# Inducing-point attention with a one-expert MLP on one Trainium2 core: second-pass weights exponentiated where the matmul leaves them, and gates of the last batch in sets of three groups

## The chip, the cores and the metric

One NeuronCore of a Trainium2 chip. The metric is device microseconds (us) of one execution; the kernel before has a median of 232.93 us over 3 runs (232.25 to 233.02). Everything is float32.

## The reference

Four batches of 11456 tokens with 128 features, and 32 inducing points. Two attention blocks follow each other, then a mixture of 8 experts:

```
h   = softmax(I @ x.T / sqrt(128)) @ x          # per batch: 32 x 128
out = softmax(x @ h.T / sqrt(128)) @ h          # per token, over the 32 rows of h
logits = out @ w_gate ; e = argmax(logits) ; gate = max softmax(logits)
y   = gate * (relu(out @ w1[e]) @ w2[e])
```

The inputs make the softmaxes nearly flat, so that all tokens of a batch take the same expert, and no hidden unit changes its sign within a batch. The kernel uses both: per batch it folds the expert into a 32-row matrix L, so that a token's output is (its 32 weights) @ L, scaled by a gate and the weights' sum. It checks what it assumes on the chip, and a flag sends it to a general path (`general_path`) where a check fails.

## The kernel before, in words

A batch is cut into 6 groups: five of 16 tiles of 128 tokens, and a last one of 10 tiles, two of them short. There are 24 groups in all.

**Pass 1** (`p1`, L393 on) per group: TensorE transposes the tiles (L404), a copy moves them from PSUM to `xT` (L406, through the helper at L317), four matmuls make the 32 scores of each token (L424), VectorE takes a maximum over each partition's scores (L431), TensorE spreads it (L435) and VectorE reduces it to one bias for each quadrant of 32 partitions (L438), ScalarE exponentiates (L442), VectorE transposes (L446), TensorE sums the weighted tokens (L453).

**Chain** (`chain`, L488) once per batch: combines the groups (L503 to L523), picks the expert (L527 to L533), gathers its weights by two indirect DMAs from GpSimd's queue (L539), and makes L (L574 to L598). L574 reads `w1e` through a view whose inner step is 8 floats.

**Pass 2** (`p2`, L607) per group: four matmuls make scores (L616) into one PSUM bank; VectorE transposes them in 32x32 blocks so that tokens lie on partitions (L618), takes each token's maximum (L620) and subtracts it (L622); ScalarE exponentiates in SBUF (L626); TensorE transposes back, four tiles at a time (L643); a copy moves the result to `eT` (L651); TensorE multiplies by L (L671); copies bring the products to `ys` (L713) and the group's gate is worked out (`gates`, L738: seven small instructions); GpSimd, ScalarE or VectorE scale (L724, L726), and a DMA stores (L734). In the last batch the logits have a matmul of their own (L654), so that the gates need not wait for L, the products are scaled straight out of PSUM (L702, L704) or, some of them, copied to `ya` and scaled by GpSimd (L695); it makes a set of gates for each group, and its stores go out four tiles at a time.

**Order.** All work is given to `Plan` (L130) as operations with a cost per engine, a key for their order, and the tiles that they open. `Plan.emit` runs a list scheduler over planned costs when the program is built; what it puts out is each engine's fixed order. It picks the engine too, where an operation names several (`Alt`), under offsets in `BIAS`. `BUFS` gives the buffers: 7 of `xT`, 6 of `x`. PSUM has 8 banks, and each tile that a matmul writes holds one until its last reader is done. SyncE issues the loads and stores in order.

Of the kernel before, what the change touches and what calls it, by code (L numbers as in the profile page):

```python
# [36 lines left out]
TM = 88  # L37
NMAIN = TM * 128
# [4 lines left out]
SCALE = 1.0 / math.sqrt(C)  # L43
OWN = -256.0
LAG = 7.38    
K1 = (-0.92, -2.62, -13.3, 1.06)
K2 = (-2.16, -2.56, 9.73, 0.73, 0.61, -2.99)
KC = -3    
XB = 0.58    
XR = 0.09      # L50
XS = 0.17    
XU = 0    
XV = 0    
XP = 50    
XW = 3
XG = 50    
XQ = (1, 1, 1, 2, 1, 0)
XH = 4
BIAS = {"tx": {"dve": 800, "act": -200}, "aT": {"dve": 100, "act": -300}, "hp": {"dve": 200, "act": -300}, "gq": {"dve": -100, "act": -100}, "s2s": {"dve": 500, "act": -200}, "eT": {"dve": 200, "act": 0}, "ys": {"dve": 0, "act": -100}, "eh": {"act": 0, "dve": 300}, "lo": {"pool": 0, "dve": 800, "act": 100}, "s1": {"pool": -200, "dve": 0, "act": -100}, "ld": {"pool": 1500, "dve": 0, "act": 50}, "yo": {"pool": 500, "dve": 300, "act": 500}, "s2s+": {"dve": -100, "act": 1500}, "eT+": {"dve": 0, "act": 50}, "ys+": {"dve": 0, "act": 50}, "eh+": {"act": 0, "dve": 200}, "lo+": {"pool": 0, "dve": 1500, "act": 50}, "s1+": {"pool": -200, "dve": -200, "act": 0}, "ld+": {"pool": 100, "dve": 0, "act": -200}, "yo+": {"pool": -200, "dve": 800, "act": 800}, "yy": {"dve": -100, "act": 100}, "hc": {"dve": 0, "pool": -300}, "yq": {"dve": 300, "act": 50}}
BUFS = {"w1e": 1, "w2e": 1, "x": 6, "xT": 7, "eT": 6, "sd": 4, "a": 1, "aT": 1, "ys": 3, "yo": 2}  # L60
# [3 lines left out]
def inducing_moe_kernel(ctx: ExitStack, tc: tile.TileContext, x, inducing, w_gate, w1, w2, out):  # L64
# [7 lines left out]
    def views(a, b, g):  # L72
        if g < G - 1:
            return [(0, 128, 0, 16, a[b, :NMAIN].rearrange("(p t) c -> p t c", t=TM)[:, g * 16:g * 16 + 16])]
        return [(0, 128, 0, 8, a[b, :NMAIN].rearrange("(p t) c -> p t c", t=TM)[:, 80:88]),
                (0, 64, 8, 10, a[b, NMAIN:NMAIN + 128].rearrange("(p q) c -> p q c", q=2)),
                (64, 128, 8, 9, a[b, NMAIN + 128:].rearrange("(p q) c -> p q c", q=1))]

# [11 lines left out]
    dve.memset(selx, 1.0)  # L90
# [12 lines left out]
    far = consts.tile([128, 128], F32, name="far")  # L103
    dve.tensor_scalar(far, sel4, 1e30, -1e30, op0=OP.mult, op1=OP.add)
# [13 lines left out]
    chk = consts.tile([128, B * G + B * NJ], F32, name="chk")  # L118
    flag = consts.tile([1, 1], I32, name="flag")

# [9 lines left out]
class Plan:  # L130
# [14 lines left out]
    WINDOW = 100  # L145
    SWITCH = 95

    def __init__(self):
        self.ops, self.tiles, self.pull, self.mode = [], {}, [], []
        self.log = []  # L150

# [3 lines left out]
    def op(self, engs, fn, r=(), w=(), key=0.0, hold=(), pull=0.0, mode=0):  # L155
# [7 lines left out]
    def emit(self, bufs, banks, run):  # L163
        n = len(self.ops)
        preds, users = [set() for _ in range(n)], {}
        writers, readers = {}, {}
        for i, (_, _, r, w, _, hold) in enumerate(self.ops):
# [16 lines left out]
        on = [None] * n  # L184
        left = {x: len(u) for x, u in users.items()}
        order = {}
        for i, (_, _, _, w, _, hold) in enumerate(self.ops):
            for x in w + hold:
                if x in self.tiles and self.tiles[x][0] != "bank":
# [6 lines left out]
        free_at = {t: [0.0] * bufs[t] for t in order}  # L196
        done, opened, last = [0.0] * n, {}, [[] for _ in range(banks)]
        bank_free = [0.0] * banks
        bank_of, bank_used = {}, [False] * banks
        clock = {"pe": 1100.0, "dve": 5300.0, "act": 2000.0, "sp": 1800.0}  # L200
        ready, cold, busy, mode = {i for i in range(n) if not need[i]}, 0.0, [], 0

        def slots(i):

            t, taken, more = [], [], []
            for x in self.ops[i][3] + self.ops[i][5]:
                if x not in self.tiles or x in opened:
                    continue
                tag = self.tiles[x][0]
                if tag == "bank":  # L210
                    k = pick(x, taken)
                    if k is None:
                        return None
                    taken.append(k)
                    t += last[k]
                else:
                    k = slot(tag, [u for g, u in more if g == tag]) if nxt[tag] + sum(g == tag for g, _ in more) == turn[x] else None
                    if k is None:
                        return None
                    more.append((tag, k))  # L220
                    t += users.get(holder[tag][k], ())
            return t

        def slot(tag, taken=()):

            free = [(free_at[tag][k], k) for k, y in enumerate(holder[tag]) if (y is None or not left[y]) and k not in taken]
            return min(free)[1] if free else None

        def pick(x, taken=()):

            allowed = range(4, banks) if x[0] == "y" else range(4) if any(self.mode[j] == 2 for j in ready) else range(banks)
            free = [k for k in allowed if not bank_used[k] and k not in taken]
            return min(free, key=lambda k: bank_free[k]) if free else None

        while ready:
            cand = []
            for i in ready:
                s0 = slots(i)
                if s0 is None:
                    continue  # L240
                for e, c in self.ops[i][0].items():
                    if e == "pe":
                        c *= 1.015
                    free = clock.get(e, 0.0) + (self.SWITCH if e == "pe" and self.mode[i] != mode else 0)
                    st = max([free] + [done[p] + self.edge(on[p], e) for p in s0]
                             + [done[p] + self.edge(on[p], e) for p in preds[i]])
                    if e == "pe" and (st < cold or st - clock[e] > 2200):
                        c *= 2
                    cand.append((st + getattr(self.ops[i][0], "bias", {}).get(e, 0.0) - self.pull[i], st, self.ops[i][4], i, st + c, e))
            first = min(cand)  # L250
            _, i, _, st, en, e = min((k, i, f, st, en, e) for f, st, k, i, en, e in cand
                                     if e == first[5] and f <= first[0] + self.WINDOW)
            engs, fn, r, w, _, hold = self.ops[i]
# [34 lines left out]
            for q in succs[i]:  # L288
                need[q] -= 1
                if not need[q]:  # L290
                    ready.add(q)
# [637 lines left out]
```

## Time and profile before

| | |
|---|---|
| median of 3 runs | 232.93 us (232.25 to 233.02) |
| the profiled execution's own time | 234.33 us |
| its span, first to last instruction | 232.5 us |
| mean granted TensorE clock | 0.900 |
| busy: TensorE, VectorE, ScalarE, GpSimd | 203.3, 175.0, 156.9, 75.8 us |
| read from and written to memory | 27.68 and 23.46 MB |

Busy is the time in which an engine had an instruction in work. For TensorE it is modelled, since its matmuls are pipelined. The profile's own time is 1.8 us over its span, and 1.4 us over the median of the runs.

### The profile page before, as it was taken

To read this page: it belongs to the slowest core of one execution; us is meant where nothing else is said; L and a number is where in the kernel's file an instruction comes from. 1 tells how busy PE (TensorE), PEld (TensorE's weight loads), DVE (VectorE), ACT (ScalarE), POOL (GpSimd) and SP (SyncE) were. 2 spreads that over 40 slices of the span, in tenths; PEclk is the share of its full clock that TensorE was granted. 3 is DMA by queue.
4 is the path that set the end of the run, shared out by engine and by line. 5 is a ranking of instruction groups with operands and counts; after the bars stand their busy time and mean duration, and the time that the engine had idled before them with its cause. 6 is when DMAs were issued, how large, how long until landed. Compare 5 with 4: busy or idle time off the path is not lost.

```text
span 232.5 us, 6577 instructions
## 1 busy us (share of the span) xinstructions
PE 203.3 (87%) x2510; PEld 135.4 (58%) x2510; DVE 175.0 (75%) x583; ACT 156.9 (67%) x429; POOL 75.8 (33%) x92
## 2 busy tenths in 40 slices
PE   8499997999999799899989989799989897799900
PEld 6277675457667474565766646375664365688700
DVE  4123284768489899998798899979897999987820
ACT  3268682186789778888976787696976876875410
POOL 2000000300014546853040477730157547712500
PEclk9979998599999999999999999999997998556655
DMA  6995759914337964959798086362005941866790
GB/s 206 375 407 206 273 180 379 307 59 123 94 149 234 395 230 169 382 206 401 223 307 318 9 259 285 148 261 66 4 39 191 312 185 66 341 240 227 266 336 25
DMA packets 12313, 51.65 MB, mean 222 GB/s; under 512 B 1617, under 2 KB 2673, under 8 KB 7921
## 3 DMA queue, kind: packets, MB, share of 16 engines
q1 hardware_dynamic: 11120, 46.95, 54.3%
q0 software_dynamic: 1152, 4.19, 5.9%
q8 instruction: 22, 0.36, 0.7%
q14 instruction: 19, 0.15, 0.2%
HBM read 27.68 MB, written 23.46 MB: 220 GB/s over the span
## 4 chain that ended last, share of the span: by engine, by line
PE 45%; DVE 36%; ACT 4%; issue 4%; DMA 3%; POOL 2%; SPq 1%; DVEq 0%; POOLq 0%; ACTq 0%
PE b L404 13%; PE b L453 7%; PE b L424 6%; PE b L671 6%; PE b L616 5%; DVE ys L317 4%; DMA x<-in_x_dram 3%; DVE sd L618 3%; DVE mx L620 3%; DVE sd L622 3%; DVE ld L749 2%; PE b L643 2%; DVE aT L446 2%; DVE mx L431 2%; PE b L435 1%
## 5 line engine op out<-in xcount | busy, mean ns | idle before, releaser
L726 POOL TENSOR_TENSOR yo<-ys,gs 128x512 f32<-128x512 f32 (+1 forms) x50 | 54.1, 1102 | 31.4 <-issue 14.2
L317 ACT COPY xT<-b 128x512 f32<-128x512 f32 (+1 forms) x92 | 49.1, 593 | 21.2 <-PE b L404 20.9
L404 PE MATMUL b<-ident,x 128*128 128x128 f32 x352 | 50.2, 289 | 3.8 <-DMA x<-in_x_dram 2.5
L404 PEld LDWEIGHTS b<-ident,x 128*128 128x128 f32 x352 | 41.4, 148 | 17.1 <-issue 7.5
L671 PE MATMUL b<-L,eT 32*128 32x137 f32 (+1 forms) x720 | 40.6, 325 | 1.1 <-DVE ys L317 0.6
L671 PEld LDWEIGHTS b<-L,eT 32*128 32x128 f32 x720 | 31.1, 206 | 17.7 <-issue 6.5
L317 ACT COPY ys<-b 128x274 f32<-128x274 f32 (+1 forms) x97 | 31.3, 388 | 9.0 <-PE b L671 7.4
L616 PE MATMUL b<-xT,hT 128*32 128x512 f32 (+1 forms) x192 | 26.6, 650 | 0.8 <-DVE sd L618 0.8
L453 PE MATMUL b<-x,aT 128*32 128x128 f32 x704 | 24.4, 277 | 1.6 <-DVE aT L446 1.2
L424 PE MATMUL b<-xT,IT 128*32 128x512 f32 (+2 forms) x192 | 24.1, 573 | 0.5 <-ACT xT L317 0.5
L746 POOL TENSOR_SCALAR s<-ys 128x16 f32<-128x16 f32 (+1 forms) x16 | 5.4, 340 | 57.2 <-DVE hp L484 24.1
L453 PEld LDWEIGHTS b<-x,aT 128*32 128x32 f32 x704 | 18.4, 110 | 8.1 <-PE b L424 1.9
L446 DVE STREAM_TRANSPOSE aT<-a 128x512 f32<-128x512 f32 (+1 forms) x24 | 16.1, 670 | 7.1 <-ACT a L442 6.6
L431 DVE TENSOR_REDUCE mx<-b 128x1 f32<-128x512 f32 (+1 forms) x24 | 15.4, 641 | 7.6 <-PE b L424 7.3
L618 DVE STREAM_TRANSPOSE sd<-b 128x512 f32<-128x512 f32 (+1 forms) x24 | 16.0, 668 | 4.9 <-PE b L616 4.9
L622 DVE CUSTOM_DVE_ANT_0 sd<-mx,sd 128x512 f32<-128x512 f32 (+1 forms) x24 | 19.0, 792 | 0.1
L442 ACT ACTIVATE a<-b,nb 128x512 f32<-128x512 f32 (+1 forms) x24 | 16.3, 678 | 4.0 <-DVE nb L438 4.0
L724 ACT ACTIVATE yo<-ys,gs 128x128 f32<-128x128 f32 x56 | 17.8, 399 | 0.9 <-ACT ys L317 0.8
L539 POOL DMA_INDIRECT w1e<-in_moe_w_dram,idx x4 | 4.4, 1101 | 41.1 <-DVE ei L535 39.7
L317 DVE COPY ys<-b 128x274 f32<-128x274 f32 x41 | 16.7, 427 | 0.8 <-PE b L671 0.7
L626 ACT ACTIVATE sd<-sd 128x512 f32<-128x512 f32 (+1 forms) x24 | 14.5, 615 | 3.1 <-DVE dst L622 3.0
L643 PE MATMUL b<-ident,sd 128*128 128x128 f32 (+1 forms) x92 | 15.3, 303 | 0.2 <-ACT sd L626 0.2
(189 smaller groups left out, 272.8 us busy)
## 6 DMA issues: line engine op xcount, KB each, us to landing
x<-in_x_dram SPq DMA_DIRECT2D x19, 1024.0 KB, 5.4
out_dram<-yo SPq DMA_DIRECT2D x15, 1024.0 KB, 4.3
out_dram<-ys SPq DMA_DIRECT2D x12, 256.0 KB, 3.4
out_dram<-yo SPq DMA_DIRECT2D x10, 256.0 KB, 2.7
x<-in_x_dram SPq DMA_DIRECT2D x4, 512.0 KB, 5.6
out_dram<-yo SPq DMA_DIRECT2D x3, 512.0 KB, 3.8
x<-in_x_dram SPq DMA_DIRECT2D x4, 256.0 KB, 3.4
xtail<-in_x_dram SPq DMA_DIRECT2D x4, 64.0 KB, 5.5
```

What stands on the lines that cost most here:

```text
L317: (eng.copy if eng is nc.scalar else eng.tensor_copy)(out, in_)
L404: e.transpose(T[t][:, k, :], xtile(i, t0 + k), ident) for k in range(n)],
L424: e.matmul(T[t][32 * k:32 * k + 32, :ends[k]], IT, T[xT][:, k, :ends[k]], start=True, stop=True) for k in range(4)],
L431: e.tensor_reduce(T[mx], T[t][:, :nt], axis=AX.XY, op=OP.max)
L446: plan.op({"dve": vec(w)}, lambda e: e.transpose(T[aT][:, :nt], T[a][:, :nt]), r=[a], w=[aT], key=base + K1[2], pull=pull)
L453: e.matmul(T[th][32 * k:32 * k + 32, :], T[aT][:n, q + k], xtile(i, q + k)[:n], start=q == 0, stop=q + k + 4 >= nt)
L616: e.matmul(T[tS][32 * k:32 * k + 32, :nt], hT, T[xT][:, k, :nt], start=True, stop=True) for k in range(4)],
L618: plan.op({"dve": vec(w)}, lambda e: e.transpose(T[s2][:, :nt], T[tS][:, :nt]), r=[tS], w=[s2], key=base + K2[0])
L622: plan.op({"dve": vec(w) + 10}, lambda e: e.tensor_tensor_reduce(out=T[sd][:, :nt, :], in0=T[mx][:, :nt].unsqueeze(2).to_broadcast([128, n ...
L643: e.transpose(T[t][:rows(a), a, :], T[sd][:, 4 * a:min(4 * a + 4, nt)].rearrange("p t m -> p (t m)"), ident)
L671: e.matmul(T[t[k]][:, a - q0, :], T[eT][32 * k:32 * k + 32, a, :], T[L][32 * k:32 * k + 32, :width], start=True, stop=True)
L726: e.tensor_mul(T[yo][:, t0:t0 + n], yv()[:, t0:t0 + n, :C], T[gs][:, t0:t0 + n].unsqueeze(2).to_broadcast([128, n, C]))
```

## The change

Pass 2 no longer brings the tokens to the partitions. The scores are made against `hq`, which is h less its mean, already multiplied by the scale; VectorE takes the largest absolute score of each partition, then of each quadrant of 32 partitions, and ScalarE exponentiates out of PSUM into `eT` with that as its bias. It writes `eT` in order, and reads the bank with an inner step of 32 floats. The transposes back and the copy to `eT` are gone. The tokens' places in a group are chosen so that this works: a load's partition holds 16 tokens in a row, a store's runs are of 4 tokens (2 in the last group). Pass 1 spreads its maximum by a VectorE transpose and four small matmuls. The gates' constant 1 is a ninth column of the exponentials. In the last batch one set of gates serves three groups, and stores are two to a group. The first three groups are loaded in four pieces each. The planner's constants, costs, buffers and offsets are new; it fills the gaps that it plans on TensorE with matmuls on ones. The core of the diff:

```diff
-BUFS = {"w1e": 1, "w2e": 1, "x": 6, "xT": 7, "eT": 6, "sd": 4, "a": 1, "aT": 1, "ys": 3, "yo": 2}
+BUFS = {'w1e': 1, 'w2e': 1, 'x': 5, 'xT': 9, 'eT': 5, 'a': 1, 'aT': 1, 'ys': 3, 'yo': 2}
+FILL = (320, 200)
+GL = 3
+EARLY = 3
...
+            if e == "pe" and st - clock[e] > FILL[0] and ops[i][0][e] > 60:
+                k = [k for k in range(banks) if not bank_used[k] and bank_free[k][1].get(e, 0.0) < clock[e] + 150]
+                if k:
+                    self.fill[i] = (max(k, key=lambda k: bank_free[k][0]), st - clock[e] - FILL[1])
...
+        if i < EARLY:
+            for t0 in range(0, 16, 4):
+                plan.op({"sp": 650}, lambda e, t0=t0: part(e, t0), key=i - 3 + 0.01 * t0,
+                        w=[("x", i), ("x", i, t0)] + ([] if i or t0 < 12 else ["ind"]))
...
-        plan.op({"pe": 109}, lambda e: e.transpose(T[tm], T[mx].to_broadcast([128, 128]), ident), r=[mx], w=[tm],
...
+        plan.op({"dve": 110}, lambda e: e.transpose(T[mm], T[mx].to_broadcast([128, M])),
...
+            e.matmul(T[tm][32 * k:32 * k + 32, :], T[mm], v["r4"], start=True, stop=True) for k in range(4)],
...
+        plan.op({"dve": 75}, lambda e: e.tensor_reduce(T[nb][:, g:g + 1], T[tm], axis=AX.X, op=OP.min),
...
-            w1v = T[w1e].rearrange("p (f j) -> p j f", j=NJ)
+            w1v = T[w1e].rearrange("p (f j) -> p f j", j=NJ)
...
+        def largest(e):
+            e.tensor_reduce(dst[:, b, g:g + 1], T[tS][:, :nt], axis=AX.XY, op=OP.max, apply_absolute_value=True)
+            e.transpose(T[mq], dst[:, b, g:g + 1].to_broadcast([128, 32]))
+            e.tensor_reduce(T[nq], T[mq], axis=AX.X, op=OP.max, negate=True)
...
+        def weights(e):
+            n = nt // 4 * 4
+            e.activation(T[eT][:, :n].rearrange("p (s i) j -> p s (i j)", i=4).rearrange("p s (j i) -> p s j i", i=4),
+                         T[tS][:, :n].rearrange("p (s i) j -> p s j i", i=4), AF.Exp, bias=T[nq])
+            for t in range(n, nt + nt % 4, 2):
...
+                e.activation(T[eT][:, t:t + 2], T[tS][:, n:nt], AF.Exp, bias=T[nq])
...
-        plan.op({"dve": vec(w)}, lambda e: e.transpose(T[s2][:, :nt], T[tS][:, :nt]), r=[tS], w=[s2], key=base + K2[0])
...
-            e.transpose(T[t][:rows(a), a, :], T[sd][:, 4 * a:min(4 * a + 4, nt)].rearrange("p t m -> p (t m)"), ident)
...
+            if o == GL - 1:
+                gates(i - o, 16 * o + 4 * ns, lambda: T[st], 0, [(st, k) for k in range(GL)], [st], base + K2[3], "+")
...
+                        for s in range(0, ns, 2):
+                            s1 = min(s + 2, ns)
+                            e.tensor_mul(part(yo, q, s, s1), part(ys, q, s, s1)[:, :, :C], times(q, s, s1))
...
+        step = 2 if last else 4
+        for q in range(0, 4, step):
+            def store(e, q=q):
+                e.dma_start(out=main[:, q:q + step], in_=yv()[:, q:q + step, :sm])
```

The check for the general path also asks that exp(-2 d) of the largest score d is at least 0.02 (`LEAST`).

## Rows read from the trace of the kernel before

**Rows 1.** Busy time of each engine in three stretches, with granted clock and DMA share
```profile
core 0: us, PE busy (x) PEld busy (x) DVE busy (x) ACT busy (x) POOL busy (x), PEclk, DMA share, GB/s
41.00:60.00 19.00, 19.00 (x177) 10.70 (x177) 13.51 (x43) 11.40 (x24) 2.11 (x2) 0.86 0.49 167
60.00:222.00 162.00, 148.98 (x1938) 99.39 (x1936) 144.30 (x479) 122.90 (x354) 72.07 (x79) 0.92 0.59 216
222.00:232.50 10.50, 0.00 (x0) 0.00 (x0) 0.28 (x1) 0.00 (x0) 0.00 (x0) 0.50 0.47 161
```

**Rows 2.** The chain that ended last, by engine and by line, from the page
```profile
PE 45%; DVE 36%; ACT 4%; issue 4%; DMA 3%; POOL 2%; SPq 1%; DVEq 0%; POOLq 0%; ACTq 0%
PE b L404 13%; PE b L453 7%; PE b L424 6%; PE b L671 6%; PE b L616 5%; DVE ys L317 4%; DMA x<-in_x_dram 3%; DVE sd L618 3%; DVE mx L620 3%; DVE sd L622 3%; DVE ld L749 2%; PE b L643 2%; DVE aT L446 2%; DVE mx L431 2%; PE b L435 1%
```

**Rows 3.** Busy time as in rows 1, of the last 26 us of work alone
```profile
196.00:222.00 26.00, 23.13 (x230) 19.51 (x230) 22.31 (x76) 16.85 (x51) 11.19 (x13) 0.57 0.71 270
```

**Rows 4.** Groups of instructions that pass 2 loses: count, busy us, mean ns, idle before
```profile
L618 DVE STREAM_TRANSPOSE sd<-b 128x512 f32<-128x512 f32 (+1 forms) x24 | 16.0, 668 | 4.9 <-PE b L616 4.9
L620 DVE TENSOR_REDUCE mx<-sd 128x16 f32<-128x512 f32 (+1 forms) x24 | 15.4, 641 | 0.1
L622 DVE CUSTOM_DVE_ANT_0 sd<-mx,sd 128x512 f32<-128x512 f32 (+1 forms) x24 | 19.0, 792 | 0.1
L626 ACT ACTIVATE sd<-sd 128x512 f32<-128x512 f32 (+1 forms) x24 | 14.5, 615 | 3.1 <-DVE dst L622 3.0
L643 PE MATMUL b<-ident,sd 128*128 128x128 f32 (+1 forms) x92 | 15.3, 303 | 0.2 <-ACT sd L626 0.2
L317 ACT COPY eT<-b 128x512 f32<-128x512 f32 (+2 forms) x19 | 10.3, 571 | 1.9 <-PE b L643 1.7
L317 DVE COPY eT<-b 128x512 f32<-128x512 f32 (+2 forms) x9 | 3.9, 457 | 0.5 <-PE b L643 0.5
```

**Rows 5.** Line L618 alone, from 60 us on: us, DVE busy (count), clock, DMA
```profile
60.00:222.00 162.00, 13.18 (x20) 0.92 0.59 216
```

**Rows 6.** Groups that price what the change adds: columns as in rows 4
```profile
L431 DVE TENSOR_REDUCE mx<-b 128x1 f32<-128x512 f32 (+1 forms) x24 | 15.4, 641 | 7.6 <-PE b L424 7.3
L471 DVE TENSOR_REDUCE nb<-nb 128x1 f32<-128x5 f32 x4 | 0.6, 154 | 0.1
L594 DVE COPY lq<-b 128x128 f32<-128x128 f32 x4 | 1.0, 258 | 0.8 <-PE b L591 0.8
L442 ACT ACTIVATE a<-b,nb 128x512 f32<-128x512 f32 (+1 forms) x24 | 16.3, 678 | 4.0 <-DVE nb L438 4.0
```

**Rows 7.** Pass 1's bias, and the gates: columns as in rows 4
```profile
L438 DVE CUSTOM_DVE_ANT_0 so<-b,far 128x128 f32<-128x128 f32 x24 | 6.6, 275 | 7.4 <-PE b L435 7.2
L748 DVE RECIPROCAL r<-s 128x16 f32<-128x16 f32 (+1 forms) x18 | 4.1, 229 | 2.1 <-POOL s L746 2.1
L749 DVE CUSTOM_DVE_ANT_1 ld<-ys,r 128x128 f32<-128x128 f32 (+1 forms) x18 | 7.8, 434 | 0.5
L753 ACT ACTIVATE le<-ld 128x128 f32<-128x128 f32 (+1 forms) x18 | 5.4, 306 | 6.7 <-DVE far__94 L749 6.7
L754 DVE TENSOR_REDUCE gs<-le 128x16 f32<-128x128 f32 (+1 forms) x18 | 4.6, 262 | 1.0 <-ACT le L753 1.0
L755 DVE SCALAR_TENSOR_TENSOR gs<-gs,s 128x16 f32<-128x16 f32 (+1 forms) x18 | 5.5, 306 | 0.1
```

**Rows 8.** Chain in order of time: start us, us, what
```profile
48.26 0.86 PE b L424 x8
...
52.98 0.92 PE b L574 x8
...
160.40 0.68 PE b L671 x16
...
206.01 2.02 PE b L671 x32
```

**Rows 9.** Timeline of PE's second load wait: start, us, instruction, idle before
```profile
11.24 1.25 PE L404 MATMUL b<-ident,x 128*128 128x128 f32 x8 [2.52 <-DMA x<-in_x_dram]
```

More of the change, by code (lines that the diff above doesn't have):

```diff
@@ L195, in emit @@
         holder = {t: [None] * bufs[t] for t in order}
[L196 to L201, printed above, removed]
+        free_at = {t: [(0.0, {})] * bufs[t] for t in order}
+        bank_free = [(0.0, {})] * banks
@@ new lines, in schedule @@
+        opened, bank_of, bank_used = {}, {}, [False] * banks
+        engines = ("pe", "act", "dve", "pool", "sp", "none")
+        clock = {"pe": 1100.0, "dve": 5300.0, "act": 2000.0, "sp": 1800.0, "pool": 0.0, "none": 0.0}
+        ready, mode = {i for i in range(n) if not need[i]}, 0
+        wide = sum(self.mode[i] == 2 for i in ready)
+        others = sum(any(self.tiles[x][0] == "bank" and x[0] != "y" for x in t) for t in opens)
+        at = [{e: 0.0 for e in engines} if not need[i] else None for i in range(n)]
@@ new lines, in schedule, with after, pick @@
+        done, on, plan = [0.0] * n, [None] * n, []
+        def after(some):
+            return {e: max((done[p] + self.edge(on[p], e) for p in some), default=0.0) for e in engines}
+        def pick(x, taken):
+            allowed = range(KEEP, banks) if x[0] == "y" and others else range(banks - KEEP) if wide and x[0] != "y" else range(banks)
+            free = [k for k in allowed if not bank_used[k] and k not in taken]
+            return min(free, key=lambda k: bank_free[k][0]) if free else None
@@ L222, in slots @@
-            return t
[L224 to L233, printed above, removed]
+                elif nxt[tag] + len(taken) != turn[x]:
+                    k = None
+                else:
+                    free = [(free_at[tag][k][0], k) for k, y in enumerate(holder[tag])
+                            if (y is None or not left[y]) and k not in taken]
+                    k = min(free)[1] if free else None
@@ L269, in emit @@
+            others -= any(self.tiles[x][0] == "bank" and x[0] != "y" for x in opens[i])
+            on[i], done[i], clock[e] = e, en, en
+            plan.append((i, e, st, en, t))
+            if i in place:
+                line.remove(i)
             if e == "pe":
                 mode = self.mode[i]
-                busy = [(a, z) for a, z in busy if z > st - 3400] + [(st, en)]
-                if st > 6000 and sum(z - max(a, st - 3400) for a, z in busy[:-1]) < 1300:
-                    cold = st + 3000
@@ L275, in emit @@
-            clock[e] = en
-            done[i] = en
-            for x in set(r) | set(w) | set(hold):
+            for x in set(ops[i][2]) | set(ops[i][3]) | set(ops[i][5]):
                 if x in left:
@@ L729, in p2 @@
                         key=key, hold=[ys])
[L730 to L736 removed]
+        sm = 4 if ns == 4 else 2
```

503 lines of the change are left out of this document (265 added, 238 removed).

## The prediction, made before the change was run

> **What bounds the kernel now.** I read the busy time by stretches first. From 60 us on, when both passes run side by side, to the last compute at 222 us, VectorE is busy 144.3 of 162 us (89%) and ScalarE 122.9 (76%): together 267.2 us, or 1.65 engines' worth. TensorE shows 149.0 (92%), but its ends are modelled. Until 60 us TensorE is busy throughout (19.00 of 19 us from 41 us on) [rows 1]. The chain that ended last says the same in another way: 45% of the span lies on TensorE and 36% on VectorE, and three lines of pass 2 on VectorE hold 3% each [rows 2]. So there are two near-bounds, and time goes down only as far as both do. In the last 26 us before 222 both are again near full (TensorE 23.1 us, VectorE 22.3), and there the granted clock is 0.57, so mostly at the lower of its two levels, 1.2 GHz [rows 3]. Behind 222 us only stores drain, 10.5 us at a DMA share of 0.47 [rows 1].
>
> **What pass 2 loses, from 60 us on.** VectorE's transpose, maximum and subtraction are 16.0 + 15.4 + 19.0 = 50.4 us, ScalarE's exponential in SBUF 14.5 [rows 4]. The transpose has 13.18 of its 16.0 us behind 60 us [rows 5], a share of 0.82, which I take for all four: 41.3 on VectorE, 11.9 on ScalarE. The copies to `eT` are 10.3 + 3.9 = 14.2 us [rows 4] and all come behind 60 us, since they wait for a chain's first exponentials. Removed: 67.4 us.
>
> **What it gains, in the 20 of 24 groups behind 60 us** [rows 5]. The maximum out of PSUM is the operation of L431, 641 ns: 12.8 us. The transpose of 32 columns and the second maximum are small: between 154 ns (a reduction of 5 columns) and 258 ns (a copy of 128); at 32 columns and less the lower is nearer: 2 x 20 x 0.154 = 6.2 us, up to 10.3. The exponential out of PSUM with a bias is L442's, 678 ns: 20 x 0.678 = 13.6 us [rows 6]. A last group issues three activations and not one; the two small ones at 306 ns (an exponential of 128 columns or fewer) [rows 7] are 4 x 2 x 0.306 = 2.4 us. Added: 35.0 us.
>
> The exponential's read has an inner step of 32 floats, which no ScalarE row of before shows. The bounds are 678 ns (L442, the same shape, engine and source, in order) and twice that. The second end is from TensorE: L574 streams 4 x 256 columns with a step of 8 floats in 0.92 us, while L424 streams 4 x 512 columns in order in 0.86, so a step cost TensorE a factor of two, out of SBUF [rows 8]. I take 678, since it shares everything but the step. The Trainium skill ("Advanced Engine Details and Errata", section "PSUM Cachelines") says that PSUM is fetched in lines of two floats and that a non-contiguous pattern significantly slows matmuls; it names no ScalarE figure, and read onto this instruction it would put the price at the upper end.
>
> **Gates.** In the last batch six sets become two. One set costs VectorE the two reciprocals (229 each), 434, 262 and 306 ns, and ScalarE 306 [rows 7], so four fewer save 1.77 x 4 = 7.1 us. The two that stay are three times as long: three instructions with 256 more elements, at about the 1.25 ns per element of L620 (641 / 512) [rows 4], add 2 x 3 x 0.32 = 1.9. Saved: 5.2 us. Multiplying in place of L755 (306 ns) is costed at no change; where it goes to GpSimd, VectorE gains up to 5.5 us.
>
> **Sum for VectorE and ScalarE:** 67.4 + 5.2 - 35.0 = 37.6 us of 267.2. At the same 1.65 engines that is 22.8 us.
>
> **TensorE** loses the transposes back, 15.3 us [rows 4]. It gains two tile slots in each of 4 last groups, 16 instructions at 0.68 / 16 us [rows 8]: 0.7. So 149.0 falls by 14.6 to 134.4; at the same 92% the stretch shrinks by 15.9 us, less than the other engines allow. What else it can win is the clock: the same 32 instructions of the products are 2 x 0.68 us earlier and 2.02 at the end [rows 8], so of 23.1 us [rows 3] some 7 are due to the lower level. Shorter waits between VectorE and TensorE in pass 2 (two crossings fewer), a lighter VectorE and the fillers should win back half, 3.5 us. Then TensorE needs 131 us, and a share of 95%, up from 92%, makes 138 of 162: 24 us. The two reckonings meet at 23 us, and I take that.
>
> **The start.** TensorE waits 2.52 us for the second group's load [rows 9], issued whole behind the first. In four pieces the first tiles come earlier, and I take the 2.5 us. Eight more issues pass through SyncE's queue ahead of the fourth group's load; at the wait that this group has now they cost nothing, and if its load came late as the second did, the 2.5 us are lost again.
>
> **Costed at nothing.** Pass 1's bias: on VectorE two small operations (2 x 154 ns [rows 6]) for one of 275 [rows 7]; four small matmuls for a transpose on TensorE. GpSimd's scaling in halves: GpSimd has 90 of 162 us free [rows 1]; without that cover it would cost the added instruction each time. Stores in runs of 4 tokens where a partition had 16 in a row: DMA is 0.59 busy [rows 1], 0.71 at the end [rows 3], so even a store at half the rate is covered until the end, where at worst the 10.5 us drain [rows 1] grows by half, 5 us; at best, with fewer issues, it shrinks by 1. Two stores on ScalarE's queue in the very last group delay what stands behind them there, the last scalings, by under 1 us. Kept in the range. Waiting for three groups before any gate in the last batch delays its first output; VectorE and ScalarE have the products and other groups' weights to do meanwhile, and without them a group's pass 2 of about 7 us (162 / 24) would show once.
>
> **Sum.** 234.33 (the profiled execution, 232.5 span and 1.8 around) - 23 - 2.5 = 208.8. That execution lies 1.4 us above the median of 232.93, so against the median: **207 us**.
>
> **Rivals.**
> *TensorE holds the gain back (0.20).* The fillers don't lift the clock and its share stays at 92%: -15.9 - 2.5 gives 234.33 - 18.4 - 1.4 = 214.5. For it: TensorE is first on the chain, 45% [rows 2], and everything it keeps (transposes, scores, products) stays. Against: many of its waits end at a VectorE line that goes.
> *More than the sum (0.17).* With 9 buffers of `xT` instead of 7 the passes overlap further, and the lighter engines reach 1.75 engines' worth: (267.2 - 37.6) / 1.75 = 131.2, so -30.8; with the start 234.33 - 33.3 - 1.4 = 199.6, and 196 where TensorE's clock also stays up (the other 3.5 us). For it: ScalarE had 24% free. Against: TensorE would have to be at 97% and more.
> *The stepped read costs double (0.06).* 20 x 0.678 = 13.6 us more on ScalarE: (37.6 - 13.6) / 1.65 = 14.5, so 234.33 - 14.5 - 2.5 - 1.4 = 215.9. For it L574; against it that L574 is TensorE out of SBUF [rows 8].
> *Slower: the bank that is exponentiated is held too long (0.06).* The scores' bank was free after one VectorE instruction of 668 ns [rows 4]; now it is held through a maximum (641), two small ones (308) and an exponential (678) [rows 6], and the wait in ScalarE's line between them: 1.0 us more at least. There are 8 banks, and every TensorE block needs one. If TensorE waits for a bank at each of 24 groups, each us of it costs 24 us; from 26 / 24 = 1.08 us per group on it eats the gain, and at 1.5 us the time is 207 + 36 = 243. Against: the bank for the transposes back is not needed any more, held through a transpose (303 ns) and a copy (571) or longer before [rows 4].
> *It doesn't do what it says (0.02).* The new check fails and the general path runs after all: times beyond any range here. For the drawn inputs the largest score less its mean is about 0.0001, where the check allows about 2, so only a flaw could do it.
>
> **Numbers.** The forecast has 0.49, with 202 to 212 as its own range (5.5 / 1.65 us less if GpSimd takes the multiplications, 4.1 / 1.65 more if the small ones cost 258 ns, the rest for the drain). The first rival adds up to 217, the second down to 196: 196 to 217 leaves out the slow case, the failing check, half of the doubled read and the far end of the second, about 0.15 to 0.2. About 0.3% is what a measurement of this kernel can tell from no change (its three runs lie within 0.33%). Faster by more: all but the last two rivals, 0.92; within: 0.01, from the held bank near its turning point; slower: 0.07.
>
> **What the profile after would show.** L618, L620, L626, L643 and the `eT` copies gone; VectorE's busy time 175 down to about 140, ScalarE's near 150; TensorE's from 203 to about 185, and a share in the shared stretch of 95%; an exponential near 0.68 us (1.3 speaks for the doubled read); no load wait over 1 us before the second group; granted clock above 0.57 in the last stretch. VectorE and ScalarE both under 75% with TensorE's sequencer waiting on ScalarE would speak for the held bank. I am wrong if the shared stretch shrinks although the busy times don't, or the other way round.

## The result, and the profile after

The changed kernel takes **203.47 us** (median of 4 runs, 201.55 to 205.67) against 232.98 for the kernel before beside it (4 runs, 232.25 to 233.28): a ratio of 0.871 [0.864, 0.878]. A second set of runs, beside which the kernel before took 230.76, gave 204.20 and 0.883 [0.877, 0.889] (e9_same below). So the gain is 27 to 30 us; the forecast was 26 (207 us, range 196 to 217). Below a difference of about 1.2% in a ratio I read nothing. In the sets of runs further down the kernel before spreads from 226.7 to 234.2 us, the runs at a granted clock of about 0.90 being the long ones (232.6 us and more) and those at 0.92 and above the shorter ones (231.7 at most), and its profile here has 0.900, so a few us between the two profiles can be its state and not the change.

The profiled execution took 202.91 us, its span is 201.1 (before 234.33 and 232.5), its mean granted clock 0.953 (before 0.900). First the page after: span, busy time of the engines, and the chain that ended last by engine and by line, which answers to [rows 2].

```profile
span 201.1 us, 6889 instructions
...
PE 180.6 (90%) x2678; PEld 126.2 (63%) x2678; DVE 155.0 (77%) x548; ACT 137.5 (68%) x375; POOL 85.7 (43%) x164
...
PE 56%; DVE 17%; DMA 13%; ACT 7%; issue 3%; SPq 1%; ACTq 0%; POOL 0%; DVEq 0%; POOLq 0%
PE b L461 14%; PE b L513 9%; PE b L716 8%; DMA w1e<-in_moe_w_dram,idx 8%; PE b L482 6%; PE b L684 6%; DMA x<-in_x_dram 5%; PE f L357 3%; DVE yo L775 3%; PE b L722 2%; DVE ys L775 2%; ACT yo L792 2%; ACT ys L362 1%; ACT xT L362 1%; PE b L498 1%
```

VectorE lost 20.0 us and ScalarE 19.4 (from 175.0 and 156.9). VectorE's share of the chain halved, from 36% to 17%, and the three lines of pass 2 that stood there are gone. In their place stands DMA with 13%, which was 3%: 8 of it the gather of the expert's first weights, `w1e`, which was not on the chain's list before.

Busy time by stretches, with granted clock, DMA share and GB/s last, as in [rows 1, 3]. The shared stretch ends at 192 us, where the last output is scaled (191.9 us; 222.3 before); only the check of the assumptions and the drain of the stores lie behind it:

```profile
core 0: us, PE busy (x) PEld busy (x) DVE busy (x) ACT busy (x) POOL busy (x), PEclk, DMA share, GB/s
41.00:60.00 19.00, 19.00 (x349) 13.33 (x336) 15.87 (x55) 14.55 (x37) 2.06 (x5) 1.00 0.51 179
60.00:192.00 132.00, 122.01 (x1852) 86.39 (x1844) 114.36 (x399) 98.07 (x288) 79.70 (x144) 0.96 0.73 267
166.00:192.00 26.00, 23.67 (x316) 19.20 (x308) 21.92 (x55) 11.31 (x32) 14.27 (x20) 0.88 0.81 300
176.00:192.00 16.00, 13.67 (x241) 11.84 (x239) 13.80 (x29) 7.04 (x19) 6.40 (x6) 1.00 0.85 317
192.00:201.00 9.00, 1.04 (x5) 0.66 (x5) 1.12 (x7) 0.20 (x1) 0.00 (x0) 0.53 0.50 168
```

The shared stretch went from 162 to 132 us, 30 less; 4.9 of these are the earlier start (table below), since the mark at 60 us stays. TensorE's share is 122.01 / 132 = 92%, as before [rows 1], and VectorE and ScalarE together do 212.4 us of work in it, 1.61 engines' worth for 1.65. So the engines are about as full as before. The granted clock in the last 26 us is 0.88 where it was 0.57 [rows 3]. The DMA queues are fuller: 0.73 for 0.59.

The new operations, and those that VectorE took over; columns as in [rows 4], the two exponentials (L696, L503) by their full form alone:

```profile
L689 DVE TENSOR_REDUCE dst<-b 128x1 f32<-128x512 f32 (+1 forms) x24 | 15.3, 638 | 1.5 <-PE b L684 1.2
L690 DVE STREAM_TRANSPOSE mq<-dst 128x32 f32<-128x32 f32 x24 | 5.1, 212 | 0.8
L691 DVE TENSOR_REDUCE nq<-mq 128x1 f32<-128x32 f32 x24 | 4.5, 186 | 1.4
L696 ACT ACTIVATE eT<-b,nq 128x512 f32<-128x512 f32 x20 | 14.0, 700 | 3.9 <-DVE nq L691 2.0 <-PE b L716 1.1 <-DVE gs L837 0.7
L700 ACT ACTIVATE eT<-b,nq 128x64 f32<-128x64 f32 x8 | 2.0, 311 | 0.0
...
L503 ACT ACTIVATE a<-b,nb 128x512 f32<-128x512 f32 x20 | 13.9, 693 | 1.3 <-DVE mm L494 0.4 <-DVE ys L362 0.4
L494 DVE STREAM_TRANSPOSE mm<-mx 128x32 f32<-128x32 f32 x24 | 4.9, 205 | 0.3
L500 DVE TENSOR_REDUCE nb<-b 128x1 f32<-128x4 f32 x24 | 3.6, 151 | 5.9 <-PE b L498 5.8
...
L362 DVE COPY xT<-b 128x512 f32<-128x512 f32 (+1 forms) x11 | 7.3, 660 | 1.5 <-PE b L461 1.4
L362 DVE COPY hp<-b 128x128 f32<-128x128 f32 x20 | 5.8, 290 | 6.5 <-PE b L513 5.4 <-PE b L498 0.9
...
L357 PE MATMUL f<-ones 128*128 128x128 f32 (+3 forms) x76 | 12.2, 306 | 0.0
```

The exponential whose read steps by 32 floats (L696) takes 700 ns for 512 columns; the same size read in order (L503) takes 693. With the smaller forms of the last groups the means of the two lines are 663 and 665. The last line is the fillers.

Where the 31.4 us between the two profiled spans came from, by milestones of TensorE's timeline (the first `sw` matmul of a batch's chain, L519 before and L578 after, and the end of the last product). "Batch" is from one chain to the next:

| kernel | first chain | batch 1 | batch 2 | batch 3 | last chain to last product | drain |
|---|---|---|---|---|---|---|
| before | 37.7 | 43.4 | 46.4 | 46.4 | 47.1 | 11.5 |
| after | 32.8 | 36.4 | 42.2 | 42.0 | 36.4 | 11.4 |

The start gives 4.9 us, the three batches 15.7, the last batch's pass 2 gives 10.7, the drain nothing.

### The profile page after: what moved, and what is told of

The parts are those of the page before. It is cut to its first block, busy times and chain, and to the rows that moved or that the text cites. A ratio compares the mean times of both kernels' runs of the same rounds, so it can differ in the third digit from the quotient of the medians.

```text
span 201.1 us, 6889 instructions
## 1 busy us (share of the span) xinstructions
PE 180.6 (90%) x2678; PEld 126.2 (63%) x2678; DVE 155.0 (77%) x548; ACT 137.5 (68%) x375; POOL 85.7 (43%) x164
## 4 chain that ended last, share of the span: by engine, by line
PE 56%; DVE 17%; DMA 13%; ACT 7%; issue 3%; SPq 1%; ACTq 0%; POOL 0%; DVEq 0%; POOLq 0%
PE b L461 14%; PE b L513 9%; PE b L716 8%; DMA w1e<-in_moe_w_dram,idx 8%; PE b L482 6%; PE b L684 6%; DMA x<-in_x_dram 5%; PE f L357 3%; DVE yo L775 3%; PE b L722 2%; DVE ys L775 2%; ACT yo L792 2%; ACT ys L362 1%; ACT xT L362 1%; PE b L498 1%
## 5 line engine op out<-in xcount | busy, mean ns | idle before, releaser
L797 POOL TENSOR_TENSOR yo<-ys,gs 128x256 f32<-128x256 f32 x106 | 62.0, 616 | 11.9 <-DVE gs L838 9.3
L362 ACT COPY xT<-b 128x512 f32<-128x512 f32 (+1 forms) x81 | 43.7, 589 | 13.8 <-PE b L461 13.3
L461 PE MATMUL b<-ident,x 128*128 128x128 f32 x352 | 47.6, 282 | 1.1 <-DMA x<-in_x_dram 1.0
L716 PE MATMUL b<-L,eT 32*128 32x137 f32 (+1 forms) x736 | 35.6, 301 | 2.2 <-DVE ys L362 2.1
L716 PEld LDWEIGHTS b<-L,eT 32*128 32x128 f32 x736 | 26.4, 186 | 11.0 <-issue 5.2
L684 PE MATMUL b<-xT,hq 128*32 128x512 f32 (+1 forms) x192 | 24.1, 592 | 0.1
L696 ACT ACTIVATE eT<-b,nq 128x512 f32<-128x512 f32 (+1 forms) x24 | 15.9, 663 | 7.0 <-DVE nq L691 5.1
L503 ACT ACTIVATE a<-b,nb 128x512 f32<-128x512 f32 (+1 forms) x24 | 16.0, 665 | 1.6 <-DVE mm L494 0.4
L689 DVE TENSOR_REDUCE dst<-b 128x1 f32<-128x512 f32 (+1 forms) x24 | 15.3, 638 | 1.5 <-PE b L684 1.2
L357 PEld LDWEIGHTS f<-ones 128*128 128x128 f32 x76 | 10.6, 213 | 2.8 <-DVE gs L838 1.7
L357 PE MATMUL f<-ones 128*128 128x128 f32 (+3 forms) x76 | 12.2, 306 | 0.0
```

What stands on the lines that cost most here:

```text
L357: self.by["pe"].matmul(t[:, :w], self.ones, self.ones[:, :w], start=True, stop=True)
L362: (eng.copy if eng is nc.scalar else eng.tensor_copy)(out, in_)
L461: e.transpose(T[t][:, k, :], xtile(i, t0 + k if g < G - 1 else order(g)[t0 + k]), ident) for k in range(n)],
L503: plan.op({"act": acc(w) + 190}, lambda e: e.activation(T[a][:, :nt], T[t][:, :nt], AF.Exp, bias=T[nb][:, g:g + 1], scale=SCALE, accum_out ...
L684: e.matmul(T[tS][32 * k:32 * k + 32, :nt], T[hq], T[xT][:, k, :nt], start=True, stop=True) for k in range(4)],
L696: e.activation(T[eT][:, :n].rearrange("p (s i) j -> p s (i j)", i=4).rearrange("p s (j i) -> p s j i", i=4), T[tS][:, :n].rearrange("p (s ...
```

## The experiments

The ratios are to the kernel before on the same chip. What an edit costs is given as a stretch between its distance from 0.883 and that from 0.871, at 231 us to 1.0.

### The removed work, put back

Theory: the gain is the removed work, worth its sum over 1.65 engines. Rival: VectorE or TensorE is in the path by itself, and its work counts in full; or the plan and not the work makes the gain.

**e2_vector_back** gives VectorE two more instructions for each group, with the order of everything else kept:

```diff
         def largest(e):
+            e.transpose(junk[:, :w], T[tS][:, :nt])
+            e.tensor_reduce(T[nq], junk[:, :384], axis=AX.X, op=OP.max)
```

> The changed kernel, order kept, with two VectorE instructions of 512 and 384 columns ahead of pass 2's maximum in each group (about 1.15 us a group, 27 us in all, what pass 2 lost there). If VectorE and ScalarE together still set the time (1.65 engines): 27 / 1.65 = 16 us more, 218 to 222. If TensorE and transfers set it now and VectorE has slack (77% busy): under 6 us more, 204 to 209.

**e3_tensor_back** gives TensorE the four transposes of a group, into the scores' bank ahead of the scores:

```diff
         plan.op({"pe": 1.7 * w + 100 * (nt < 16)}, lambda e: [
+            e.transpose(T[tS][:, 4 * k:4 * k + 4], T[xT][:, k, :4], ident) for k in range((nt + 3) // 4)] and [
             e.matmul(T[tS][32 * k:32 * k + 32, :nt], T[hq], T[xT][:, k, :nt], start=True, stop=True) for k in range(4)],
```

> The changed kernel, order kept, with pass 2's transposes of 128 columns back on TensorE (four a group, 92 in all, about 0.44 us a group), written into the scores' bank ahead of the scores. If TensorE is the near-bound of the changed kernel (90% busy, 56% of its chain): 8 to 12 us more, 211 to 216. If VectorE and ScalarE are: under 4 us more.

**e4_all_back** makes both edits and adds a ScalarE copy to `eT`:

```diff
         def weights(e):
             n = nt // 4 * 4
+            e.copy(T[eT][:, :nt], T[tS][:, :nt])
```

> Both of these and a ScalarE copy of 512 columns a group (0.57 us) besides: nearly all the engine work that pass 2 lost, in the changed kernel's order and buffers. If the removed work made the gain, as the prediction has it: 25 to 33 us more, 228 to 237. If the new order, buffers and lag made most of it: 215 or less.

**e5_old_plan** keeps every new operation and goes back to the planner's constants, keys, offsets and buffers of before (7 of `xT`, 6 of `x`, no fillers), by the planner of before:

```diff
-FILL = (320, 200)
...
-BUFS = {'w1e': 1, 'w2e': 1, 'x': 5, 'xT': 9, 'eT': 5, 'a': 1, 'aT': 1, 'ys': 3, 'yo': 2}
+BUFS = {"w1e": 1, "w2e": 1, "x": 6, "xT": 7, "eT": 6, "a": 1, "aT": 1, "ys": 3, "yo": 2}
```

> All operations of the changed kernel, but ordered by the planner of before with its keys, windows, offsets and buffers (7 of xT, 6 of x, banks split between products and the rest, no fillers). If the removed work made the gain whatever the order: 203 to 212. If order, lag and buffers made a good part of it: 215 to 228. If the held bank needs the new order: above 228.

Measured: e2 227.26 us, 0.987 [0.978, 0.996]; e3 211.89, 0.920 [0.912, 0.929]; e4 227.31, 0.988 [0.978, 0.998]; e5 212.33, 0.924 [0.915, 0.934]. From the pages, the engines' busy time and the chain by engine of e2, then the busy time of e4:

```profile
PE 191.6 (86%) x2678; PEld 133.2 (60%) x2678; DVE 180.5 (81%) x596; ACT 138.1 (62%) x375; POOL 85.6 (38%) x164
...
DVE 42%; PE 38%; DMA 6%; ACT 6%; issue 4%; ACTq 0%; POOL 0%; DVEq 0%; POOLq 0%
```

```profile
PE 198.8 (88%) x2770; PEld 136.4 (61%) x2770; DVE 180.4 (80%) x596; ACT 150.1 (67%) x399; POOL 85.6 (38%) x164
```

| kernel | first chain | batch 1 | batch 2 | batch 3 | last chain to last product | drain |
|---|---|---|---|---|---|---|
| e2 | 32.6 | 43.3 | 46.8 | 45.0 | 43.5 | 11.6 |
| e4 | 32.7 | 43.4 | 48.7 | 45.5 | 42.7 | 11.8 |
| e5 | 35.9 | 40.2 | 43.2 | 41.9 | 39.7 | 8.6 |

In e2 VectorE is busy 25.5 us longer, and the kernel is 24 us longer by the ratio of e9 (27 by the first one; the profiled spans differ by 21.7). That is more than either branch of what was expected: VectorE's work counts nearly in full, and DVE leads the chain at 42%. The first three batches take as long as they did before the change, within 1.4 us. TensorE's (e3, 10.2 us more busy) costs 8.5 to 11 us when it is alone, so that counts in full too. But e4, which adds both and ScalarE's 12.6 us, costs no more than e2: what TensorE and ScalarE do more is covered by the time that VectorE takes anyway. That is two near-bounds side by side, as read from [rows 1]; the division by 1.65 is not what comes out for VectorE's part in this fixed order. Two reservations. The order was made without the added work, so an addition may cost more here than its removal brought. And the granted clock moves too: in e2 it is 0.928 (after: 0.953), and TensorE, with the same 2678 instructions, is busy for 191.6 us and not 180.6; in e4, with 92 instructions more on TensorE, it is 0.965. So part of what e2 costs may come by way of the clock, and part of what e4 adds may be covered by a better one; these runs do not part the two.

e5 gives the new operations (loads in pieces and gates in sets among them) without the new plan: 0.924, 17.5 us of the gain. The remaining 9 to 12 us come with the new plan, its buffers and its fillers. With the old plan the second and third batch are hardly slower than after; 3.1 us up to the first chain, 3.8 in batch 1, 0.9 in the next two and 3.3 at the end are what the new plan is worth, and the drain gives 2.8 back. The two parts don't simply add: with the old work back, the new order gives less than 3 us (e4, 0.988).

### Fillers, loads in pieces, gates in sets

**e1_nofill** leaves the fillers out and nothing else:

```diff
-        n = int(ns / 1.667) // 32 * 32
+        n = 0
```

> The changed kernel, its order and engines kept, with the 76 filler matmul instructions (12.2 us of TensorE) left out. If the fillers won back clock, as the prediction took for half of 7 us: the mean granted clock falls from 0.953 towards 0.90, the products of the last batch slow down, and the time rises by 2 to 5 us (205 to 209). If they only stand in gaps that are there anyway: the same within 1 us. If they stand in the way of real blocks (3.2% of the chain after): 1 to 5 us less.

Measured: 209.70 us, 0.909 [0.898, 0.921], so 6 to 9 us more. Three stretches of e1, the second to be held against the same 176 to 192 us above, the third from the last chain to the last product:

```profile
117.00:158.00 41.00, 36.65 (x565) 24.88 (x568) 31.61 (x121) 31.01 (x93) 21.11 (x42) 0.88 0.51 186
176.00:192.00 16.00, 11.08 (x193) 8.32 (x192) 12.15 (x31) 5.64 (x16) 9.54 (x14) 0.79 0.72 266
155.50:197.00 41.50, 33.78 (x406) 22.99 (x406) 31.56 (x99) 22.05 (x67) 25.56 (x40) 0.79 0.63 234
```

And the kernel after from its last chain to its last product, as the third line of e1:

```profile
153.30:189.70 36.40, 35.90 (x471) 26.81 (x469) 31.04 (x98) 21.39 (x66) 25.43 (x40) 0.91 0.70 262
```

Up to the third chain (111.9 us, after: 111.4) the two kernels agree. Then TensorE waits for the gather in both, and the clock falls; from 117 to 158 it is 0.88 in e1 and 0.96 after. In 176 to 192 it is 0.79 where the kernel after has 1.00. Of the 7.3 us between the two spans the third batch has 1.6 and the stretch from the last chain to the last product 5.1 (41.5 us for 36.4, at a clock of 0.79 for 0.91). The products' line L716 takes 40.4 us in all for 35.6. The fillers, 12.2 us of TensorE, win more than they take.

**e7_whole_loads** loads the second and third group whole, at the place of their first piece:

```diff
-            e.dma_start(out=T["x", i][:, t0:t0 + 4], in_=views(x, b, g)[0][4][:, t0:t0 + 4])
+            if i == 0 or t0 == 0:
+                n = 16 if i else 4
+                e.dma_start(out=T["x", i][:, t0:t0 + n], in_=views(x, b, g)[0][4][:, t0:t0 + n])
```

> The changed kernel, order kept, but groups 1 and 2 loaded whole, as before, instead of in four pieces. By the prediction the pieces gave 2.5 us: 205 to 207, with a load wait of over 2 us before the second group's transposes. If the first batch's pass 1 has slack behind it: within 1 us of 203.

Measured: 208.80 us, 0.903 [0.891, 0.915]: 4.6 to 7.4 us more. The first chain begins at 36.3 us and not 32.8, 3.5 us later, and the last product ends 5.3 us later than after. TensorE's one wait for a load, as it was to show:

```profile
PE b L463 <- DMA x<-in_x_dram: 2.8, 1, 2.8
```

So the pieces are worth 3.5 us at the start; the rest is lost on the way and within what I read.

**e8_gates_single** makes a set of gates for each group again; the planner makes a new order for it:

```diff
-GL = 3
+GL = 1
```

> The changed kernel with a set of gates for each group of the last batch (planned anew under the same constants). By the prediction the sets of three save 5.2 us of VectorE and ScalarE, 3 us of time: 205 to 208. If VectorE has slack in the last batch or the sets' waiting eats it: 203 or less.

Measured: 210.21 us, 0.918 [0.912, 0.925], 8 to 11 us more. VectorE is busy 1.7 us longer and ScalarE 2.4, 4.1 in sum. The last chain begins at 154.8 us (after 153.3) and the last product ends 44.6 us later, where it was 36.4. In that tail the new plan has seen gaps and filled them:

```profile
L357 PE MATMUL f<-ones 128*128 128x128 f32 (+3 forms) x146 | 19.1, 280 | 0.3 <-DVE ys L775 0.3
```

Twice the fillers of after: the plan leaves TensorE more gaps. From the last chain to the last product the clock is 0.92 (after: 0.91), so it is not the clock that makes this tail longer. Since the order is another, the 8 us belong to the sets and to the order that they allow; how much is the 4.1 us of work, this run does not tell.

### The transfers, which now wait

Theory: the gather of `w1e` stands in the queues with a load of 1 MB and is late, because in the kernel after the same bytes pass in less time. The first half is borne out in part below, the second is not. SyncE's own timeline, and TensorE's, at the gathers that go out at 76.07 and 118.22 us:

```profile
75.13 6.65 SPq L428 DMA_DIRECT2D x<-in_x_dram  x2
...
83.47 0.67 PE L635 MATMUL b<-w1e,hT 128*32 128x256 f32 x8 [1.25 <-DMA w1e<-in_moe_w_dram,idx]
...
117.27 6.66 SPq L428 DMA_DIRECT2D x<-in_x_dram  x2
...
127.14 0.67 PE L635 MATMUL b<-w1e,hT 128*32 128x256 f32 x8 [2.76 <-DMA w1e<-in_moe_w_dram,idx]
```

The chain of the kernel after, in order of time, and its stretches there (columns as above):

```profile
76.07 7.27 DMA w1e<-in_moe_w_dram,idx
...
118.22 8.79 DMA w1e<-in_moe_w_dram,idx
```

```profile
79.00:84.00 5.00, 3.75 (x64) 1.48 (x56) 4.69 (x16) 3.30 (x9) 3.59 (x8) 1.00 1.02 408
125.00:130.00 5.00, 2.86 (x23) 2.20 (x24) 1.80 (x7) 1.73 (x6) 1.36 (x3) 0.77 1.03 402
```

The DMA engines are busy throughout there (shares of 1.02 and 1.03), and in the second stretch TensorE is busy for 2.9 of 5 us and every other engine for less than 2. The median landing of the gather went from 4.2 to 6.8 us, that of the 1 MB loads from 5.4 to 6.7.

The place in the order is what differs from before. In the kernel after, a store and a load of 1 MB go out 1.4 and 0.9 us ahead of each of these two gathers. In the kernel before, SyncE issues nothing in the 3.5 us ahead of the gathers of the same batches (84.71 and 132.65 us), and they land in 4.3 and 4.2 us at a DMA share of 0.58. The shorter time alone doesn't make a gather late: e2 keeps the order of after, takes 227 us with the same bytes at a DMA share of 0.66 in its shared stretch (60 to 213 us), and its second and third gather land in 7.5 and 8.7 us all the same, with shares of 1.03 and 0.99 around them. The gather's landing before:

```profile
DMA to landing us min/median/max: 4.2/4.2/4.4
```

In e2, with TensorE's wait for it (us in total, times, longest), which is no less than the 4.0 us after:

```profile
DMA to landing us min/median/max: 4.6/7.0/8.7
...
PE b L636 <- DMA w1e<-in_moe_w_dram,idx: 4.2, 2, 2.7
```

And e5, faster than before by 18 us under the old plan, has no wait for a gather on TensorE; there they land in 5.3 to 6.6 us.

**e6_quarter_stores** stores a quarter of each group outside the last batch and leaves out the rest:

```diff
-                e.dma_start(out=main[:, q:q + step], in_=yv()[:, q:q + step, :sm])
+                n = step if last else 1
+                e.dma_start(out=main[:, q:q + n], in_=yv()[:, q:q + n, :sm])
```

> The changed kernel, order kept, but of the first three batches only the first quarter of each group's main store is written (13 MB of 23.5 MB are left out). If the gathers of the experts' weights (6.8 us to landing against 4.2 before) and the loads now wait in a full DMA queue, and TensorE behind them: gathers land in 5 us or less, and the time falls by 5 to 10 us (193 to 198). If these waits are covered: within 2 us of 203.

Measured: 195.50 us, 0.853 [0.847, 0.859], 4 to 7 us less. The gather's row on its page (median us from issue to landing last), and the chain by engine:

```profile
PE 64%; DVE 20%; ACT 5%; DMA 3%; issue 3%; SPq 2%; ACTq 0%; DVEq 0%
...
w1e<-in_moe_w_dram,idx POOLq DMA_INDIRECT x4, 4.6
```

The gather lands in 4.6 us, TensorE's wait for it is gone and DMA is back to 3% of the chain. Batch 1 takes 36.4 us as after, batch 2 40.7 (42.2), batch 3 37.6 (42.0). So the traffic costs what the wait of 4.0 us says, and up to 3 more. It frees the output buffers sooner too, and the load that went out 0.9 us ahead of the gather now goes out 3.3 us ahead of it; this run doesn't tell these apart.

**e9_same** is the kernel after, unchanged, beside the next two.

> The changed kernel unaltered, on the chip of the next two, as their measure. The first measurement was 0.871 of before (0.864 to 0.878), 203.5 us: the same within 1%.

204.20 us, 0.883 [0.877, 0.889]. **e10_gather_first** lets SyncE read 4 bytes of `w1e` before it issues that load, so that it goes out only when the gather has landed; the order is the same:

```diff
-            vs = views(x, b, g)
+            vs, late_ = views(x, b, g), b and g == 3 and e.dma_start(out=junk, in_=T["w1e", b - 1][:1, :1])
```

> The changed kernel with the order of every compute engine kept; SyncE waits for the gather of the first expert matrix (by a transfer of 4 bytes that reads it) before it issues the load that the end of each batch's pass 1 sets free, which now goes out 1 us ahead of the gather. If the gather is late because that load fills the DMA queue: gathers of the second and third batch land in about 5 us instead of 7 to 9, TensorE's waits of 1.3 and 2.8 us for them and the loss of clock behind go, and the time falls by 3 to 6 us (197 to 201). If the held load then comes late itself, or if stores are what the gather meets: the same within 1.5 us, or slower.

**e11_gather_planned** tells the planner that a gather takes 7.0 us and not 4.6:

```diff
-            on({"none": 4600}, lambda e: None, [(wx, "q")], [gate])
+            on({"none": 7000}, lambda e: None, [(wx, "q")], [gate])
```

> The changed kernel, planned anew with 7.0 us instead of 4.6 for a gather's landing (6.8 is the trace's median). If the plan's too short landing leaves TensorE standing: other blocks or fillers stand in that place, no wait over 1 us for a gather is left, and the time falls by 2 to 4 us (199 to 202). If the order found is as good or bad as any, or the later L holds up the products: 202 to 207.

Measured: e10 216.53 us, 0.941 [0.935, 0.947]; e11 216.09, 0.935 [0.928, 0.941]: both 12 to 13 us slower than e9 beside them. The waits of e10 (us in total, times, longest), TensorE's and then SyncE's:

```profile
PE b L461 <- DMA x<-in_x_dram: 12.0, 5, 4.4
...
SPq L427 <- DMA w1e<-in_moe_w_dram,idx: 31.2, 3, 15.4
```

SyncE stood 31.2 us for three gathers, and everything behind in its line with it; TensorE then waited 12.0 us for loads. Its wait for the gather fell to 1.7 us, from 5.4 in e9. The second and third gather landed in 6.0 and 7.7 us, for 8.4 and 8.7 in e9 and not the 5 expected, so that load is one part of what makes them late and not the whole. It is not early either: my theory of a cheap delay fell. e11, too, is outside both branches of what was expected. No wait for a gather is left on TensorE's list, but the plan for it has 178 fillers (24.8 us), and the last chain to the last product takes 52.6 us. A better order of the transfers may exist; neither way found one, and no version here beats the kernel after with all its work.

**e12_long_runs** asks whether the shorter runs of the stores (2 KB for 8) load the queues:

```diff
+                if ns == 4 and not last:
+                    return e.dma_start(out=outb[b, 2048 * g:2048 * g + 2048].rearrange("(p t) c -> p t c", t=16), in_=T[yo][:, :16])
                 e.dma_start(out=main[:, q:q + step], in_=yv()[:, q:q + step, :sm])
```

> The kernel after, except that the stores of whole groups (15 of 1 MB by the profile) write each partition's 16 tokens as one run of 8 KB instead of four runs of 2 KB: the same bytes from the same tile at the same place in the order, but tokens stand in other rows of the output. The order of all instructions stays. Theory 1 (the gathers land late because the same bytes pass in less time): nothing changes; ratio 0.871 to 0.883, landing of w1e 6.8 to 8.4 us, its wait on TensorE about 4 us, the queue's share near 0.64. Theory 2 (shorter runs load the queues): the queue's share falls by 3% of itself or more, the landing of w1e goes back towards 4.2 us, and the time falls by 2 to 7 us, to a ratio of 0.85 to 0.87.

Measured: 202.06 us, 0.887 [0.879, 0.894], no difference from 0.883. SyncE's queue (packets, MB, share of 16 engines' span), and landings, first of e12, then of after:

```profile
q1 hardware_dynamic: 13520, 46.85, 63.6%
...
out_dram<-yo SPq DMA_DIRECT2D x15, 1024.0 KB, 4.4
...
w1e<-in_moe_w_dram,idx POOLq DMA_INDIRECT x4, 6.8
```

```profile
q1 hardware_dynamic: 19280, 46.85, 64.6%
...
out_dram<-yo SPq DMA_DIRECT2D x15, 1024.0 KB, 5.0
...
w1e<-in_moe_w_dram,idx POOLq DMA_INDIRECT x4, 6.8
```

Packets fall by 30%, the queue's time only from 0.646 x 201.1 = 129.9 us to 0.636 x 200.4 = 127.5. The stores land as they did before the change (4.4 us; 4.3 before), the gather as late as after. The run length is not the cause. With e2 that leaves the place of the large transfers ahead of the gather, which the new order set; which of them costs what is open.

## Why the prediction was right, and where its steps were off

**The sum of work was right.** Predicted were 37.6 us less on VectorE and ScalarE behind 60 us, which by the same prices is 42.8 for all 24 groups; the whole kernel shows 39.4. Putting the work back in the same order takes the gain away nearly in full (e4, 0.988).

**Its split was wrong.** The profile after was to show VectorE near 140 and ScalarE near 150; it shows 155.0 and 137.5. Two things moved: the planner gave VectorE copies that ScalarE used to make (`hp` 5.8 us, part of `xT` 7.3), and the small operations cost more than the 154 ns taken: the 32-column transposes 205 and 212 ns, the second maximum 186, inside the bound of 258 that the step kept. GpSimd took 12 of the 18 gate multiplications, as the range allowed. 24 x (212 + 186 - 308) ns is 2.2 us; with pass 1's pair, 1.1 more.

**The step from work to time** held as a number; as a mechanism it isn't confirmed. 37.6 / 1.65 = 22.8 us and TensorE's 24 met at 23; the shared stretch shrank by 30 us, 25 without the earlier start, at 1.61 engines for 1.65, and with TensorE at 92% and not 95%. The quotient fits e4, too: 38.0 us of VectorE and ScalarE work put back are 23.0 by it, and cost 24 to 27. But e2's 25.5 us of VectorE work alone cost as much, where the quotient is 15.5: the size is that of VectorE's part, two thirds of the sum, and the division meets it because of that mix. And under the old plan the same operations gave 17.5 us (e5), not the 25.5 that the sum has for work and start; the 9 to 12 us of the new plan, for which it had no term but the clock in TensorE's reckoning, made up for that. So the number is in part luck.

**TensorE** fell from 203.3 to 180.6 us busy, forecast "about 185", and that with 12.2 us of fillers in it. The clock was taken at half of 7 us, 3.5; e1 puts the fillers alone at 6 to 9. The step was too small: the products at the end [rows 8] are the larger part of it (5.1 us of e1's 7.3 lie behind the last chain), but without fillers the clock fell already in the third batch's chain, and that batch was 1.6 us longer.

**The start** was taken at 2.5 us, the wait for one load [rows 9]. The first chain came 4.9 us earlier, and e7 puts the pieces at 3.5 of these, with a wait of 2.8 us for one load. Where the other 1.4 us come from, no run shows.

**The gates** were taken at 5.2 us of work and so 3 of time. e8 shows 4.1 of work and 8 of time in the tail, with a new order; the work was about right, and what the sets alone are worth in time stays open. That work behind the last chain costs more because little else is left to hide it is my reading, and no run tests it.

**The stepped read** was taken at the price in order, and nearly is: 700 ns against 693 for 512 columns. The Trainium skill ("Advanced Engine Details and Errata", section "PSUM Cachelines") speaks of matmuls slowed by patterns that aren't contiguous in PSUM; for a ScalarE read, of which it says nothing, the trace shows no such slowing. TensorE's read of `w1e` out of SBUF did get cheaper where the order of its columns changed: eight matmul instructions in 0.67 us (timeline above), 1.10 in the same view before, both at a granted clock of 1.00.

**Transfers costed at nothing** was half right. Short runs cost nothing that can be measured in the time (e12), and the drain stayed (11.4 us after 11.5). What was missed is the gather: the new order puts a store and a load of 1 MB just ahead of it, and it lands late. The transfers in all, the gather's wait among them, cost 4 to 7 us (e6). I listed what covers a store, and not what else stands in the same queues.

**The rivals.** TensorE did hold its share of 92%, but the clock came back, so 214.5 did not come about (e1, without fillers, is 209.7). The 196 to 199.6 of the second rival is what e6 reaches (195.5) with three quarters of those stores left out: it needed the transfers out of the way, with TensorE at 95% of its shared stretch (60 to 185.5 us) and a clock of 0.99. The held bank doesn't show. TensorE's waits in the kernel after (us in total, times, longest), the first of the list and the one on the exponential:

```profile
PE b L635 <- DMA w1e<-in_moe_w_dram,idx: 4.0, 2, 2.8
...
PE b L722 <- ACT eT L696: 0.5, 1, 0.5
```

One wait of 0.5 us, in 24 groups, is all that TensorE's matmuls wait for the exponential.

## What to carry to other kernels

Work put back on the engine that then led the chain counted nearly one for one here (e2), and work on the others beside it nothing (e4); a division by a mean number of busy engines gives the right size only for the mix of work that it was read from, and an experiment that puts the work back in the same order measures it. When the order of a kernel is made anew, price the transfers anew: look for the small transfer with a short deadline (a gather that a chain waits for) and for the large ones that now go out just ahead of it. Compare stretches that end at the same event: 4 us of check behind the last output would have made TensorE's share here 90% and not 92%. Gaps that a plan leaves on TensorE were worth filling where the granted clock fell behind them (e1), and the price is seen in the stretches after the gap, not in it.

## What the runs showed of the hardware

- ScalarE reading PSUM with an inner step of 32 floats took 700 ns for 512 columns, in order 693.
- A gather of `w1e` landed in 4.2 to 4.4 us in the kernel before, at a DMA share of 0.58 around the second and third; with a store and a load of 1 MB issued 1.4 and 0.9 us ahead of it, in 7.3 and 8.8 us after and 7.5 and 8.7 in e2, at shares of 0.99 to 1.03 around it; and in a median of 4.6 with three quarters of the stores left out (e6).
- Stores of 1 MB in runs of 2 KB landed in 5.0 us and in runs of 8 KB in 4.4, with 30% fewer packets and only 2% less queue time.
- Leaving out 76 filler matmuls brought the granted clock from the last chain to the last product from 0.91 to 0.79, and that stretch from 36.4 to 41.5 us.
